# A two-stage kernel on one core: the filler products of TensorE at the start go from 26 to 44, with a new fixed order of the first half

## The chip, the cores and the metric

One Trainium2 chip, one of its cores. The metric is the device time of one launch in microseconds (us); lower is better. A core has five engines that each run their own instructions in the order of the program: PE (TensorE, matrix products, with its weight loads shown as PEld), DVE (VectorE), ACT (ScalarE), POOL (GpSimd) and SP (here it only issues transfers). Semaphores tie the engines together; an engine whose next instruction has to wait holds up everything behind it.

## What is computed

```python
# attention part: 4 batches x 8 heads, 768 steps, head size 48
k_n = k / (norm(k) + 1e-6)
for t in range(S):
    y[t]  = q[t] @ state
    v_old = state^T k_n[t]
    state = state + beta[t] * outer(k_n[t], v[t] - v_old)
# feed-forward part: x is y laid out as 3072 tokens x 384
h = x @ w_in          # 384 x 2048
g = h * cos(h)
out = g @ w_out       # 2048 x 384
```

All of it is float32. Nothing of it changes with the edit.

## The kernel before, in words

The sequence is cut into 24 units of 32 steps (`n` in the code); two units make a block of 256 tokens (`p`, 12 of them) for the feed-forward part. For each unit the recurrence is solved in closed form: `turn` (L556) transposes keys and queries on TensorE, `gram` (L588) makes their products, `gram_keys`, `fold` and `gram_queries` (L610, L631, L662) bring these out of the accumulators on VectorE, `inv` (L709) inverts a triangular matrix (on VectorE for the first pair of units, on GpSimd afterwards), `back` (L646) brings the inverse into place. Then comes the chain that runs from unit to unit: `state` (L752, keys and queries times the state), `old` (ACT), `right` (DVE), `solve_half` (L805), `half_out` (ACT), `between` (L813), `between_out` (DVE), `solve` (L825), `solve_out` (DVE, L843), `update` (L856), `update_out` (DVE, L868), which gives the state of the next unit, and beside it `within` (L874), `within_out` (ACT) and `within_rest` (DVE, both L888), which give the unit's output y. `features` (L899) transposes y, `features_out` (ACT, L909) lays it down as x. From there on the feed-forward part can use it: `hidden` (L956, x times w_in), `turns`, `rest`, `cos` and `gate` (g = h cos h on ACT and DVE), `out` (times w_out). From block 1 on the second product, and from block 2 on the first product as well, use sums of tiles to save multiplications (`layer`, `in_sums`, `right`, `left`, `collect`).

The weights come in as 64-bit words of which one float is wanted. Each of the 28 pieces takes a load on SP (`weights`, L450), two passes on ACT (`split`, L457), two on DVE (`shift`, L466) and one on POOL (`add`, L475). Four landing buffers hold the pieces, so a fifth load waits until an earlier `add` is done.

`busy` (L951) is a product of a constant tile that nobody reads. It writes to the accumulator of the output, which is not in use until the first `out`; the first `out` is ordered behind the last `busy` (L1604). One call is one product of 128x256, which the profile shows as two instructions. `BUSY` (L1303) is the number of calls.

The order of the work is not found by a scheduler at build time. All steps, with their dependencies, are registered by `order.add`, and `Order.run` (L175) issues them in the order that the list of numbers `LINE` (L54) gives; number i is the i-th step registered. The same list thus sets the order on each of the five engines, and which buffer a step gets: a tag of which all buffers are in use is passed on as soon as its last user in the list is done. Of the accumulators that matter here, `two` and `kq` exist once each, `h` three times (L1294 to L1297). Units 0, 2 and 4 are transposed and multiplied in `two`, units 1 and 3 in `kq`, so `turn` of unit 2 waits until the last reader of unit 0's products is done, and `solve_half` of unit 0 waits until the last reader of unit 2's products is done. The end of the function pins each engine's instructions to the order of issue.

The function that the list drives:

Of the kernel before, what the change touches and what calls it, by code (L numbers as in the profile page):

```python
# [54 lines left out]
0 1 2 3 4 5 6 7 2141 8 9 10 11 12 37 13 76 38 14 39 42 34 98 64 15 43 69 65 40 66 70 44 2145 45 99  # L55
67 71 2142 16 47 17 72 2143 2149 128 75 2144 2146 46 77 106 143 2153 201 129 18 101 74 19 2147 2150
20 78 2148 21 2157 165 22 102 23 79 103 2154 131 36 107 73 2155 136 2151 2156 24 137 2161 80 25 190
2158 26 132 104 27 133 28 81 2165 108 166 29 2152 109 2162 48 41 110 49 111 2169 2159 50 63 2163
2160 51 168 52 2166 169 30 2164 2173 53 191 134 54 170 31 2170 55 2167 56 2177 223 2171 58 68 2172
32 59 57 2174 60 172 2168 2181 100 138 2175 173 2176 33 139 61 142 2185 62 2189 743 171 130 144 2182  # L60
140 141 744 2178 248 82 2179 145 174 83 749 175 2183 2190 224 750 176 2191 2184 755 751 84 745 177
756 2186 2193 2192 226 2187 146 2197 85 281 746 86 87 752 747 88 748 89 2194 2188 90 753 757 227
2180 91 2198 2201 105 93 2205 2199 147 92 2195 194 94 2200 148 761 195 2209 2196 95 2202 196 758 228
2213 2206 762 197 199 198 759 2207 96 112 97 754 2210 2203 767 2208 2214 2211 200 2204 763 768 760
113 2215 2217 2212 230 2221 114 773 2225 231 2216 249 229 791 769 202 770 764 2229 135 765 167 115
2218 774 203 116 771 2222 772 117 775 779 2226 776 192 118 777 2227 204 119 766 780 120 306 121 781
2230 123 122 785 124 2219 205 782 786 125 783 339 784 126 778 149 787 127 788 252 150 2231 2220 789
819 2223 253 2228 151 820 2233 2237 2224 35 225 152 821 790 825 153 803 206 822 823 826 2241 2234
287 154 2235 827 283 831 155 824 288 156 804 2232 832 157 2242 2236 193 2238 2245 158 2243 207 833
837 364 159 828 232 834 829 160 284 792 161 233 811 835 208 162 2249 234 250 807 163 179 164 2239  # L70
2246 254 830 235 838 255 836 2250 257 843 839 2251 209 180 310 844 812 285 840 849 289 841 258 259
845 805 850 178 256 2244 2247 793 2252 846 181 847 346 2240 842 813 851 855 2248 848 898 309 182 260
852 856 183 853 854 184 210 857 251 186 286 261 794 187 185 397 899 341 900 211 795 188 868 797 212
808 262 858 859 213 901 282 214 861 215 860 216 189 902 263 218 422 904 862 219 217 905 798 909 317
863 220 903 906 221 290 815 264 345 799 311 399 342 291 292 800 222 864 912 865 809 265 866 796 312
400 801 307 237 313 907 867 314 920 923 315 921 810 870 347 266 932 293 908 934 933 911 873 924 910
938 935 914 940 874 922 939 915 238 913 941 267 916 367 936 871 876 942 937 343 925 943 872 947 926
869 236 949 878 948 944 957 239 945 950 879 816 951 316 946 880 818 802 344 368 955 806 817 240 956
881 952 882 268 241 318 953 954 242 308 244 404 960 245 243 319 884 958 917 961 455 269 959 246 962
992 270 886 927 963 971 883 320 928 887 964 271 965 403 369 272 966 888 967 273 968 247 321 930 274  # L80
931 889 969 276 480 875 970 885 277 977 972 275 890 978 278 973 979 877 814 322 891 974 279 980 975
426 348 929 375 976 295 349 981 986 892 982 919 894 280 987 323 983 988 895 918 984 350 296 893 985
989 425 998 990 896 991 370 324 993 1011 371 999 1045 373 1042 994 1006 1000 995 1007 1014 1043 996
351 1008 997 1009 1001 457 1054 1010 1002 1012 1056 1055 325 1003 401 374 297 1004 1044 1046 1058
1005 1057 1013 1062 1060 1047 1059 458 1069 1061 294 402 1071 1070 1017 1015 1063 433 1048 376 1072
340 1079 1064 1018 372 1065 405 1073 897 298 377 461 1020 299 1066 300 1074 1067 1022 302 326 1075
1016 1023 1068 303 378 1050 301 1077 365 304 327 1078 1076 1049 1080 1024 328 1053 513 1052 1019
1082 1025 379 1081 329 1026 1083 1084 330 1085 1028 331 1086 305 1087 332 1030 1088 380 366 334 538
1031 335 1089 333 1090 1029 1093 1091 336 1032 1092 1021 337 1094 1099 381 398 427 1095 406 1100 353
1096 1051 1097 407 423 1101 1033 354 1098 1034 1102 382 1027 338 1108 408 515 1103 1114 1109 1104  # L90
1035 1110 1105 462 355 1106 1111 1036 516 1038 1112 383 1107 1113 1039 459 1037 1115 409 1164 1116
1120 1167 1040 1117 428 1121 1165 1118 517 1128 1133 429 1129 1119 431 1122 1130 1131 1176 1123 352
1168 1136 1124 1132 1177 1125 1178 518 1126 432 1139 1166 1127 1180 483 1137 1179 430 1184 1182 1169
1181 1138 1191 1134 1183 1135 356 1192 434 491 1193 357 384 1185 1172 1194 1140 1170 1195 1186 484
1171 435 1187 1196 358 463 1197 360 1142 571 359 361 1198 1201 1188 436 460 1189 1199 385 1200 1190
1202 1204 1041 1144 1203 362 519 1145 1174 1205 1141 386 437 1206 1146 1175 1207 363 1208 1215 1147
520 1209 1148 1210 1211 1150 438 1149 387 1212 1152 456 1236 1213 1214 388 1216 1153 481 389 1217
1221 1218 439 485 1219 390 1222 392 596 1173 391 1223 393 1143 1154 1220 1224 440 1230 1155 1225
1156 394 1226 1231 395 1227 1157 1232 542 1151 1228 1233 573 1158 1229 1160 1234 1159 574 1235 396
1161 1237 575 464 441 465 1242 466 1238 1162 1239 486 1243 1286 467 1240 411 1250 1289 1251 1241  # L100
1244 1252 1255 487 1253 1245 489 1287 1246 1254 1258 1247 410 424 1298 1261 1248 1300 1299 1288 1249
412 490 521 1302 541 1301 1259 1304 488 1256 1262 1305 413 1303 1290 549 1291 1307 1260 1306 492 414
1308 1264 415 442 1309 1310 1313 1257 1311 493 1266 1315 1163 1314 1312 416 1316 1292 418 1317 629
1267 1318 417 1319 494 419 1323 1320 482 1321 1268 1322 1324 577 1326 1293 1325 420 1294 522 1269
1327 495 443 1328 421 523 578 1329 1270 543 1330 444 1272 524 1331 600 1337 1274 1332 496 445 1275
1333 1263 514 1334 1265 446 1335 1276 447 1336 599 1297 1338 1343 497 1277 1339 1271 448 1344 1295
525 1340 450 449 1341 1345 451 1342 539 1278 1346 1347 498 1352 1348 1279 1353 452 1354 1349 544 453
1280 1350 1355 1273 545 1282 547 546 1351 1356 1358 1296 1357 1378 454 1364 1359 1283 1365 1360 1372
548 1366 1361 1373 1284 1362 499 469 1374 1281 1367 1375 1377 1363 1408 1368 1409 1380 1376 550 1411
1369 1420 576 468 1422 1421 1370 1410 1412 1383 1371 470 551 1424 654 540 1384 1423 1413 471 1428  # L110
1386 579 1425 1426 1381 1379 472 1427 552 1435 500 473 1429 1382 1436 474 1430 635 1388 476 1431
1414 1389 1432 477 475 553 1285 1437 1385 687 1433 1387 1390 478 1438 501 1391 1439 1434 1415 1392
502 1416 1440 554 1443 1393 1441 1419 1445 1444 1442 1394 503 1446 572 1447 1448 1396 1418 1395 1397
1449 636 1450 555 504 1451 1398 505 1452 479 506 1399 1453 508 712 507 1454 556 1400 509 1455 601
1456 607 580 631 1457 1459 1458 581 510 1465 511 1460 583 632 1401 1466 1461 582 633 1467 1462 557
1417 1463 602 1468 512 527 1464 1402 603 1474 1469 1470 1404 605 1475 1471 1476 1405 1472 526 528
1473 1477 1406 1480 1478 606 1530 1486 1479 529 1481 1499 1403 1500 1487 657 1482 1531 1494 1488
1483 1495 1502 604 1484 1496 597 608 1485 1497 530 1533 1542 1498 1489 1544 1532 1407 1490 531 1543
609 1491 1505 532 637 1492 534 689 1493 693 1546 1545 1534 535 1506 1535 610 690 533 1548 1550 558
1547 1503 1508 1549 1501 665 1536 1551 1504 658 1510 1557 1552 536 559 611 1558 1509 1553 694 634  # L120
1559 560 1511 1560 1554 1561 1512 561 1555 1562 630 1556 1563 562 612 1565 1564 1513 1567 563 655
1566 1570 1538 1568 659 1514 1571 1569 537 1516 1572 613 715 1573 564 1574 1518 1575 566 1537 1576
1519 565 567 1577 614 1581 1578 568 569 1520 1579 1541 1580 1507 638 1582 1587 1517 1583 639 1584
585 1588 570 1515 1585 1589 1521 586 640 691 1539 1586 1602 1590 641 1596 1540 1591 1522 1597 615
# [76 lines left out]
def kernel(  # L201
# [1101 lines left out]
    BUSY = 26  # L1303
# [506 lines left out]
```

## Time and profile before

| what | us |
|---|---|
| three runs | 631.16, 634.62, 634.65 |
| their median | 634.62 |
| the profiled execution, whole | 634.23 |
| its span, from the first to the last instruction | 632.2 |
| TensorE products, busy in the span | 603.0 |
| VectorE, busy in the span | 545.6 |
| mean granted TensorE clock | 0.984 |

The page of the profile divides the span into 40 equal slices of 15.8 us; a digit is the busy share of an engine in tenths, and PEclk the granted clock of TensorE in tenths. The view by windows gives the same for stretches of one's own choice. The timeline lists an engine's instructions in order of time, merged when alike: start, length, engine, line, operation, tiles, number; in brackets the idle time of the engine before it and what ended it. A product in float32 counts as two instructions.

### The profile page before, as it was taken

To read this page: it belongs to the slowest core of one execution; us is meant where nothing else is said; L and a number is where in the kernel's file an instruction comes from. 1 tells how busy PE (TensorE), PEld (TensorE's weight loads), DVE (VectorE), ACT (ScalarE), POOL (GpSimd) and SP (SyncE) were. 2 spreads that over 40 slices of the span, in tenths; PEclk is the share of its full clock that TensorE was granted. 3 is DMA by queue.
4 is the path that set the end of the run, shared out by engine and by line. 5 is a ranking of instruction groups with operands and counts; after the bars stand their busy time and mean duration, and the time that the engine had idled before them with its cause. 6 is when DMAs were issued, how large, how long until landed. Compare 5 with 4: busy or idle time off the path is not lost.

```text
span 632.2 us, 24257 instructions
## 1 busy us (share of the span) xinstructions
PE 603.0 (95%) x10096; PEld 559.2 (88%) x10096; DVE 545.6 (86%) x1131; ACT 350.7 (55%) x643; POOL 345.8 (55%) x703
## 2 busy tenths in 40 slices
PE   7669799999999999999999999999999999999997
PEld 5458678877998989999999999999999999999996
DVE  6986978989999999988999998989988887878782
ACT  3644666554454756655655566755645655746340
POOL 4465787858948588387186683782680780000000
PEclk9877899999999999999999999999999999999999
DMA  9786574764454645555554445544334103110000
GB/s 180 189 215 155 140 182 107 130 101 78 85 102 82 127 77 102 99 85 104 89 87 92 92 75 112 104 72 74 70 77 82 48 17 66 34 42 22 1 26 25
DMA packets 223985, 57.60 MB, mean 91 GB/s; under 512 B 215684, under 2 KB 218900, under 8 KB 223876
## 3 DMA queue, kind: packets, MB, share of 16 engines
q1 hardware_dynamic: 221444, 55.22, 43.4%
q8 instruction: 79, 1.29, 0.9%
q10 hardware_dynamic: 2176, 0.39, 0.4%
q0 software_dynamic: 256, 0.45, 0.4%
q14 instruction: 30, 0.25, 0.1%
HBM read 42.13 MB, written 13.89 MB: 89 GB/s over the span
## 4 chain that ended last, share of the span: by engine, by line
PE 74%; DVE 10%; DMA 5%; ACT 3%; issue 2%; POOL 2%; SPq 2%; ACTq 0%; DVEq 0%
PE p_out L1226 28%; PE p_h L1149 27%; PE p_kq L764 3%; PE p_h L963 3%; PE p_s L862 3%; PE p_kq L879 2%; PE p_out L1169 2%; PE p_g L598 2%; PE p_u L841 2%; DMA pairs<-in_moe_w_in_dram 2%; DMA qp<-in_q_dram 2%; PE p_o L1226 2%; DVE p_h L1047 1%; SPq L339 1%; DVE pairs L468 1%
## 5 line engine op out<-in xcount | busy, mean ns | idle before, releaser
L734 POOL TENSOR_TENSOR part<-z,gb 128x56 f32<-128x56 f32 (+25 forms) x325 | 134.3, 413 | 113.5 <-DMA gb<-g_dr 58.1
L735 POOL TENSOR_TENSOR z<-z,part 128x56 f32<-128x56 f32 (+25 forms) x325 | 138.2, 425 | 25.5
L1165 ACT COPY g_ffn<-p_h 128x512 f32<-128x512 f32 x140 | 79.7, 586 | 90.3 <-DVE p_h L1047 49.5
L1226 PE MATMUL p_out<-w_out,g_ffn 128*128 128x192 f32 x672 | 120.9, 329 | 0.0
L1047 DVE TENSOR_TENSOR p_h<-p_h,g_ffn 128x512 f32<-128x512 f32 x140 | 97.0, 695 | 18.9 <-ACT g_ffn L1165 10.9
L1226 PEld LDWEIGHTS p_out<-w_out,g_ffn 128*128 128x128 f32 x672 | 107.9, 191 | 0.7
L1001 ACT ACTIVATE turns<-p_h,quarter_turn 128x512 int32<-128x512 f32 x96 | 65.8, 687 | 64.2 <-DVE p_h L1047 52.8
L1017 ACT ACTIVATE turns<-turns,halfpi 128x512 f32<-128x512 f32 x96 | 69.2, 722 | 46.9 <-DVE turns L1008 45.7
L1226 PE MATMUL p_out<-w_sum,g_ffn 128*128 128x192 f32 x496 | 91.2, 331 | 0.5 <-DVE p_h L1047 0.5
L1149 PE MATMUL p_h<-x_sum,w_in 128*128 128x128 f32 x640 | 83.9, 278 | 0.4 <-ACT g_ffn L1165 0.3
L1226 PEld LDWEIGHTS p_out<-w_sum,g_ffn 128*128 128x128 f32 x496 | 79.4, 190 | 2.2 <-DVE p_h L1047 0.6
L1149 PEld LDWEIGHTS p_h<-x_sum,w_in 128*128 128x128 f32 x640 | 78.1, 192 | 1.9 <-ACT g_ffn L1165 1.0
L1008 DVE SCALAR_TENSOR_TENSOR turns<-p_h,turns 128x512 f32<-128x512 f32 x96 | 65.3, 684 | 8.1 <-ACT turns L1001 7.7
L1242 DVE TENSOR_TENSOR g_ffn<-g_ffn 128x512 f32<-128x512 f32 x88 | 62.7, 722 | 4.1 <-PE p_out L1226 3.9
L1026 DVE TENSOR_TENSOR g_ffn<-turns,p_h 128x512 f32<-128x512 f32 x86 | 58.4, 680 | 6.8 <-ACT turns L1017 6.7
L1149 PE MATMUL p_h<-x_sum,in_sum 128*128 128x128 f32 x400 | 53.8, 278 | 0.7 <-DVE g_ffn L1026 0.6
L897 ACT COPY y<-p_kq 32x384 f32<-32x384 f32 x88 | 41.3, 469 | 19.0 <-PE p_kq L879 13.6
L963 PE MATMUL p_h<-x_ffn,w_in 128*128 128x128 f32 x384 | 50.3, 289 | 1.1 <-ACT x_ffn L912 0.7
L1149 PEld LDWEIGHTS p_h<-x_sum,in_sum 128*128 128x128 f32 x400 | 49.5, 192 | 2.0 <-DVE g_ffn L1026 0.6
L963 PEld LDWEIGHTS p_h<-x_ffn,w_in 128*128 128x128 f32 x384 | 46.9, 201 | 2.7 <-issue 1.1
L776 ACT COPY rhs<-p_kq 32x384 f32<-32x384 f32 x86 | 40.2, 467 | 7.8 <-issue 4.9
L1149 PE MATMUL p_h<-x_ffn,w_in 128*128 128x128 f32 x320 | 42.9, 278 | 0.1
(133 smaller groups left out, 891.4 us busy)
## 6 DMA issues: line engine op xcount, KB each, us to landing
pairs<-in_moe_w_in_dram SPq DMA_DIRECT2D x12, 512.0 KB, 3.9
pairs<-in_moe_w_out_dram SPq DMA_DIRECT2D x16, 384.0 KB, 4.2
gb<-g_dr SPq DMA_DIRECT2D x20, 256.0 KB, 3.6
vp<-in_v_dram SPq DMA_DIRECT2D x96, 48.0 KB, 2.4
out_dram<-o SPq DMA_DIRECT2D x23, 192.0 KB
y_dr<-y_t SPq DMA_DIRECT2D x20, 192.0 KB, 3.4
x_ffn<-y_dr SPq DMA_DIRECT2D x40, 96.0 KB, 2.5
kp<-in_k_dram SPq DMA_DIRECT2D x128, 24.0 KB, 2.2
```

What stands on the lines that cost most here:

```text
L734: eng.tensor_tensor(out=part, in0=row, in1=times, op=ALU.mult)
L735: eng.tensor_tensor(out=behind, in0=behind, in1=part, op=ALU.subtract)
L963: nc.tensor.matmul(p_h[:, i], w_in[:, t, (4 * k + i) * 128 : (4 * k + i + 1) * 128], moved(p, t, unit), start=(t == 0), stop=(t == KT - 1),)
L1001: nc.scalar.activation(turns[p, f], hidden_of(p, f), AF.Identity, bias=quarter_turn, scale=TURN)
L1008: nc.vector.scalar_tensor_tensor(out=r, in0=hidden_of(p, f), scalar=TURN, in1=t, op0=ALU.mult, op1=ALU.subtract,)
L1017: nc.scalar.activation(r, r, AF.Sin, bias=halfpi, scale=2.0 * math.pi)
L1026: nc.vector.tensor_tensor(out=place(p, f), in0=step_of(rests.pop((p, f)), f), in1=step_of(hidden_of(p, f), f), op=ALU.mult,)
L1047: nc.vector.tensor_tensor(out=out, in0=one, in1=two, op=ALU.add if op == "add" else ALU.subtract)
L1149: nc.tensor.matmul(p_h[:, e], in_block(w)[:, e], form(p, x), start=first and e == 0, stop=True, skip_group_check=True,)
L1165: nc.scalar.copy(block(p, *CHAIN[i][3]), p_hs[p, BANK[i]])
L1226: nc.tensor.matmul(p_o, left(p, part, a)[:, e % 4], right(e, b), start=(e == 0), stop=(e == FT // 2 - 1), skip_group_check=True,)
L1242: nc.vector.tensor_tensor(out=left(p, s, to), in0=left(p, s, one), in1=left(p, s, two), op=op)
```

## The change

`BUSY` becomes 44, which registers 18 more steps, so that every number in `LINE` from 34 on means another step. The list is written anew. Put back into names, its last 1191 entries (from about block 4 on) are the same steps in the same order as before; of the 1036 steps ahead of these that are not `busy`, 959 stand in another place, 745 of the 1036 within 10 places of the old one and 985 within 40. No step's own code is touched, and the dependencies are the same.

```
     VECTOR = {0: "h"}
-    BUSY = 26
+    BUSY = 44
...
-0 1 2 3 4 5 6 7 2141 8 9 10 11 12 37 13 76 38 14 39 42 34 98 64 15 43 69 65 40 66 70 44 2145 45 99
+0 1 2 3 4 5 6 7 2159 8 9 10 11 12 55 13 56 60 57 52 116 82 87 61 83 58 84 88 62 2163 63 117 94 85 89
...
```

In names, TensorE's order up to the features of unit 1 (BUSYxN are N products that nobody reads, `hidden.p,f,part`):

```
before: BUSYx7 turn.0 BUSYx1 turn.1 gram.0 gram.1 BUSYx2 turn.2 BUSYx6 turn.3 BUSYx5 gram.2 BUSYx1 state.0
  solve_half.0 between.0 BUSYx1 solve.0 BUSYx1 update.0 within.0 BUSYx1 turn.4 gram.3 BUSYx1 features.0
  hidden.0,0,0 hidden.0,0,1 state.1 gram.4 hidden.0,2,0 hidden.0,2,1 hidden.0,4,0 hidden.0,4,1 solve_half.1
  between.1 solve.1 update.1 within.1 turn.5 hidden.0,6,0 gram.5 hidden.0,6,1 features.1
after:  BUSYx6 turn.0 turn.1 gram.0 gram.1 BUSYx21 turn.2 BUSYx3 turn.3 BUSYx2 gram.2 BUSYx6 state.0 BUSYx2
  solve_half.0 between.0 solve.0 BUSYx2 update.0 within.0 turn.4 gram.3 features.0 BUSYx1
  hidden.0,0,0 hidden.0,0,1 hidden.0,2,0 gram.4 state.1 hidden.0,2,1 hidden.0,4,0 solve_half.1
  between.1 solve.1 hidden.0,4,1 update.1 within.1 turn.5 hidden.0,6,0 BUSYx1 gram.5 state.2 hidden.0,6,1 features.1
```

(`state.0` issues nothing: the state is zero.) VectorE's order over the same stretch, up to the end of unit 0's output:

```
before: sum.0,0 beta sum.0,1 scale.0,0 gram_keys.0 scale.0,1 gram_queries.0 gram_keys.1 shift.0 cross.0 fold.0
  inv.0,0 gram_queries.1 shift.1 inv.0,1 sum.1,0 inv.0,2 fold.1 shift.3 shift.2 inv.0,3 sum.1,1 scale.1,0 back.0
  gram_keys.2 weigh.0,0 fold.2 right.0 gram_queries.2 shift.4 shift.5 sum.2,0 between_out.0 scale.1,1 solve_out.0
  shift.6 shift.7 weigh.0,1 update_out.0 within_rest.0
after:  sum.0,0 beta sum.0,1 scale.0,0 gram_keys.0 scale.0,1 fold.0 gram_keys.1 gram_queries.0 cross.0 sum.1,0
  inv.0,0 shift.0 inv.0,1 shift.1 shift.2 scale.1,0 gram_queries.1 fold.1 shift.3 inv.0,2 sum.1,1 gram_keys.2
  inv.0,3 weigh.0,0 back.0 fold.2 gram_queries.2 right.0 shift.4 shift.5 between_out.0 shift.6 sum.2,0 scale.1,1
  solve_out.0 shift.7 update_out.0 beta_home within_rest.0
```

ACT, after `within_out.0`: before `split.8 turn_out.4 features_out.0 split.10 split.9 old.1`, after `turn_out.4 split.9 features_out.0 split.10 split.11 turns.0,0 split.12 old.1`; `split.8` now stands ahead of `within_out.0`. POOL: `norms.1,0` now stands ahead of `add.0`, `add.9` and `add.10` ahead of most of `inv.1`. SP: `q.3` now goes ahead of `k.3`, `v.0` ahead of `weights.4`, `q.5` and `q.6` ahead of `weights.8` and `weights.9`; `v.1`, `k.6` and `v.3` go later.

## The prediction

> **What bounds the kernel now.** First the page: busy times, the slices, the clock. Then windows, to see which stretch loses what; then the timelines of TensorE and VectorE over the begin.
>
> ```profile
> span 632.2 us, 24257 instructions
> PE 603.0 (95%) x10096; PEld 559.2 (88%) x10096; DVE 545.6 (86%) x1131; ACT 350.7 (55%) x643; POOL 345.8 (55%) x703
> ...
> PE   7669799999999999999999999999999999999997
> ...
> DVE  6986978989999999988999998989988887878782
> ...
> PEclk9877899999999999999999999999999999999999
> ```
>
> TensorE is the bound from the fifth slice on; only the begin has pauses and a clock below full. A gain must come from the first 100 us, and it lasts to the end, since what TensorE does earlier is not waited for again.
>
> ```profile
> 30.00:40.00 10.00, 5.38 (x195) 4.32 (x196) 9.11 (x25) 4.79 (x8) 7.52 (x5) 0.74 0.86 218
> 40.00:50.00 10.00, 7.55 (x181) 5.51 (x181) 8.44 (x20) 4.76 (x12) 5.51 (x6) 0.84 0.81 188
> 50.00:60.00 10.00, 10.00 (x179) 9.63 (x179) 5.21 (x12) 3.51 (x8) 5.74 (x16) 0.74 0.60 144
> 60.00:70.00 10.00, 6.82 (x284) 5.96 (x283) 8.39 (x16) 6.95 (x13) 8.15 (x17) 0.94 0.61 165
> ```
>
> Columns: length, busy us and instructions of PE, PEld, DVE, ACT, POOL, then granted clock, DMA share, GB/s. From 30 to 40 us VectorE is full and TensorE is not; from 50 to 60 us TensorE is full at three quarters of the clock and VectorE idles half the time. Read in half-microsecond windows, the clock is 0.5 from 17.7 to 21.1, 34.8 to 41.6, 48.4 to 55.25 and 68.9 to 72.3, and 1.0 afterwards: 20.5 us at half clock, so 10.2 us of TensorE's work lost. All edges lie multiples of 3.41 us apart.
>
> ```profile
> 13.42 1.13 PE L954 MATMUL p_out<-eye 128*128 128x256 f32 x4
> 17.71 1.08 PE L561 MATMUL p_t<-consts,kp 128*128 128x128 f32 x4 [3.16 <-DVE part_v L734]
> 25.19 0.63 PE L561 MATMUL p_t<-consts,kp 128*128 128x128 f32 x4 [1.95 <-issue]
> 26.10 2.32 PE L954 MATMUL p_out<-eye 128*128 128x256 f32 x10
> 33.91 0.88 PE L801 MATMUL p_w<-vp,halves_z 32*32 32x48 f32 x64 [4.08 <-issue]
> 46.84 0.66 PE L598 MATMUL p_g<-kq_t 48*32 48x64 f32 x41 [1.09 <-issue]
> 49.12 5.46 PE L963 MATMUL p_h<-x_ffn,w_in 128*128 128x128 f32 x24 [0.66 <-ACT x_ffn L912]
> 54.51 1.46 PE L764 MATMUL p_kq<-st,kq_t 48*64 48x48 f32 x64
> ```
>
> ```profile
> 26.54 1.52 DVE L473 TENSOR_SCALAR w_in<-w_in 128x512 uint32<-128x512 uint32 x1
> 33.41 0.40 DVE L664 TENSOR_TENSOR tt<-p_g,consts 128x256 f32<-128x256 f32 x1
> 39.73 1.02 DVE L849 TENSOR_TENSOR u<-p_u,bz 128x384 f32<-128x384 f32 x2 [0.61 <-PE p_u L835]
> 44.04 1.13 DVE L895 COPY y<-p_kq 32x384 f32<-32x384 f32 x2
> 56.79 0.42 DVE L624 TENSOR_TENSOR g<-p_g,bs 128x256 f32<-128x256 f32 x1 [4.45 <-PE p_g L598]
> ```
>
> Each of TensorE's pauses up to 44 us ends with a VectorE step: turn.2 at 17.71 follows fold.0, turn.3 at 25.19 follows fold.1 (24.81 to 25.09), solve_half.0 at 33.91 follows gram_queries.2 (33.41 to 33.81). VectorE itself waits 0.61 us for TensorE before solve_out.0 (39.73), and 4.45 us before 56.79: that is where the half clock hurts, because 24 product instructions (5.46 us; later rows of 24 at full clock take 2.9) stand ahead of state.1 and gram.4.
>
> **The change, part by part.** *The 18 added products.* Ten instructions at full clock take 2.32 us, the last one 0.38: (2.32 - 0.38)/9 = 0.216 each, 0.43 per product. At the start 14 took 6.29, so 0.85 per product at half clock. The block of 21 begins at about 13.4 and lasts 42 x 0.216 = 9.1 us, to 22.5: turn.2 comes at 22.5 instead of 17.71. Behind it on TensorE: turn.2 (0.9), 3 products (1.3), turn.3, which needs fold.1 at about 25.2 as now, so that the queue is idle again: 25.2 to 26.1; 2 products to 27.0; gram.2 to 27.8. Its reader gram_keys.2 on VectorE has inv.0,2 and sum.1,1 ahead of it and is reached at about 28.5. Slack 0.7 us: cost nothing, as long as the block runs at full clock. At half clock until the gate opens it is 1.7 to 3.4 us longer, and 1.0 to 2.7 of it would reach VectorE. The 6 + 2 products after gram.2 end at 27.8 + 8 x 0.43 = 31.2, ahead of solve_half.0. The 6 instead of 7 at the start only wait for loads less long. Of the 18, then, nothing lies on the path, and what they hold up, the clock between 17.7 and 41.6 us, is worth little: VectorE waited 0.61 us for it in all (39.73). Gain 0 to 0.6.
>
> *VectorE up to the first output.* Summing durations in both orders, the work up to gram_queries.2 is the same. But two of its rows were stretched beside a POOL add: L473 at 26.54 took 1.52 where others take 0.42, and the sum of cross.0 0.99 where cross.1's took 0.43. In the new order POOL's adds fall elsewhere (add.0 behind norms.1,0, shift.2 next to no add). Gain 0 to 1.66; I take 1.1, so solve_half.0 at 32.8. From there to the end of within_rest.0 now 11.36 us; weigh.0,1 leaves (0.47), beta_home comes (0.78), the wait of 0.61 goes, and of the second stretched L473 (35.26, 1.52) about half: 10.5 to 11.7, I take 11.2. So within_rest.0 ends at 44.0 instead of 45.17.
>
> *To the first hidden product.* Now 45.17 to 49.12 = 3.95: gram.3 with a pause of 1.09 inside it (46.84), one product, p_z, x on ACT. The product goes behind features.0 (-0.4), but split.9 (1.25) stands ahead of features_out.0 on ACT, and split.8 ahead of within_out.0. Their loads wait for landing buffers: weights.9 for the sixth add at about 37.3, and behind q.6 on SP (1.88), so 39.5; early loads took up to 7.3 us from issue to their split (13.24 to 20.53): 46.8 at worst, 44.2 by the issue at 21.45 and the next piece of the chain ending at 26.16. Taken: hidden.0 at 47.0; ends 46.0 and 49.2.
>
> *The clock under these products.* Between 37.7 and 46 us the new order leaves TensorE update, within, turn.4, gram.3, features.0 and one product: about 4.5 us of 9, longest pause about 2.2. Windows of 3.41 us ahead of the four drops held 0.3, 0.8, 2.1 and 1.5 us of busy TensorE; ones with 1.9 and more were also kept. So I expect a drop here as now, and the gate to open after a whole busy window: at about 52, half clock for some 5 us of products instead of 6.1. Gain 0.5 in TensorE's work.
>
> *Unit 1.* state.1 now comes after 12 more product instructions and gram.4: from 47.0, 22 instructions at 0.228 to 52, 14 at 0.118 to 53.7, gram.4 0.8, state.1 from 54.5 to 55.7 (now 55.97). old.1 to 56.7. right.1 was reached at 60.24 because shift.10, gram_queries.4 and shift.12 (1.02 + 0.42 + 1.81) stood between it and 56.79; now only gram_keys.4 does. right.1 at 56.8, 1.73 long, then gram_queries.4: solve_half.1 at 59.0 instead of 62.23. From there to features.1 now 14.15 us; hidden.0,4,1 put ahead of update.1 (1.4) lies beside solve_out.1 (1.1), back.1 moves behind within_rest.1 (1.8 earlier), shift.15 and sum.3,0 come ahead of it (about 1.8): nil.
>
> *Sum.* Start of hidden.0 -2.1, clock -0.5, the order after it -0.6: unit 1 stands 3.2 us earlier at features.1, and TensorE, 9 tenths or more busy from there to the end, keeps it. Later moves (in_sums, right, left, stores, loads by up to 50 places; q.3, v.0, q.5 ahead on SP and v.1, k.6, v.3 behind) I cost at nothing: by sums of durations VectorE's work ahead of features.2, update_out.5 and the products of block 2 differs by less than 3.1 us either way while TensorE's own queue is 95% full; if that cover is gone, the difference is the price. 634.23 - 3.2 = 631.0; the profiled execution is 0.39 below the median of 634.62.
>
> **A rule against it.** The row first: the drop at 48.4 came after a window (45.0 to 48.4) with 2.1 us of busy TensorE. The Trainium skill (TensorE: Matmul & The Clock Gate, What's actually happening) says that the clock goes to half after at least one idle window of about 3.4 us. By that rule this drop would not have come, so the trace disagrees here. By it the new begin, whose longest pause I put at 2.2 us, would stay at full clock: that is the first rival.
>
> **Rivals.** (1) The clock holds through the first features. For it: 1.9 us of busy TensorE in a window were sometimes enough. Against: 2.1 were not. The 24 + 12 instructions then take 4.2 instead of 6.7, and the rest of the 10.2 us lost now stays away: 631.0 - 2.5 - 1.7 (68.9 to 72.3) = 626.8. (2) Slower: state.1 behind 12 more instructions at half clock. It decides if hidden.0 does not start earlier than 49.1, through the pause of 1.09 or a late weights.9. Then 36 instructions at 0.228 end at 57.3, gram.4 0.8, state.1 at 58.1 against 54.51; VectorE's next steps wait and unit 1 is 3.6 late: 637.8, or 636 if right.1's shorter queue gives half back. (3) It does nothing: the pauses end with VectorE, which is full, and the later order gives the rest back: 634.2.
>
> **How the numbers follow.** Forecast 0.42 (its own range 629 to 633), rival 1 0.2, rival 2 0.2, rival 3 0.18. Leaving out a tenth on each side: 626.0 to 638.0. One per cent, about what a measurement of this kernel can tell from no change, is 6.3 us: faster means below 628.3, slower above 641.0. Rival 1 and the low tail of the forecast give 0.22; slower by more needs rival 2 and another unit lost the same way, 0.08; within 0.70.
>
> **What would show it.** In the new profile: turn.2 near 22.5 and gram_keys.2 without an idle bracket (the block is covered); solve_half.0 near 32.8; within_rest.0 ending near 44.0; the first hidden product near 47.0; a half clock over it but not from 17.7 to 41.6; solve_half.1 near 59; features.1 near 73. I am wrong if gram_keys.2 waits for TensorE, if hidden.0 starts at 49 or later, or if pauses on TensorE appear after 100 us that were not there.

## The result: 1.4% slower

| | us | runs |
|---|---|---|
| before | 634.37 (630.92 to 634.81) | 6 |
| after | 641.22 (637.58 to 643.87) | 6 |
| after by before | 1.0142, 95% interval 1.0111 to 1.0173 | |

The profiled execution of the changed kernel took 641.66, its span 639.9. The forecast was 631.0, its upper end 638.0. The page of the changed kernel:

```profile
span 639.9 us, 24344 instructions
PE 613.7 (96%) x10132; PEld 570.4 (89%) x10132; DVE 547.7 (86%) x1131; ACT 351.2 (55%) x643; POOL 347.9 (54%) x703
...
PE   7959889999989999999999999999999999999997
...
DVE  6986779899979999998999998989988977878782
...
PEclk7977799999989999999999999999999999999999
...
q8 instruction: 80, 1.31, 0.9%
```

TensorE has 36 more product instructions, and the clock is lower in the first and fifth slices and in the twelfth. By windows of half a microsecond it is at half from about 9.4 to 16.2, 36.7 to 43.5, 46.9 to 57.1, 67.4 to 74.2 and 183.4 to 186.9, some 34 us against 20.5. The last line becomes important below: a queue that carries instructions moved 80 packets, 1.31 MB, 16 KB each. The four stretches shown of the kernel before, now of the changed one (same columns):

```profile
30.00:40.00 10.00, 5.65 (x185) 4.51 (x187) 9.07 (x17) 4.83 (x8) 4.98 (x4) 0.83 0.83 172
40.00:50.00 10.00, 6.30 (x136) 5.10 (x135) 7.90 (x19) 2.19 (x4) 6.55 (x4) 0.67 0.79 197
50.00:60.00 10.00, 9.82 (x171) 8.62 (x170) 6.34 (x18) 6.56 (x14) 6.04 (x12) 0.64 0.44 126
60.00:70.00 10.00, 7.39 (x293) 6.76 (x281) 7.84 (x15) 5.35 (x10) 6.20 (x14) 0.87 0.57 123
```

From 40 to 50 us TensorE does 136 products where it did 181. The timeline of TensorE says why:

```profile
13.75 10.52 PE L955 MATMUL p_out<-eye 128*128 128x256 f32 x42
24.10 0.60 PE L562 MATMUL p_t<-consts,kp 128*128 128x128 f32 x4
...
28.10 0.86 PE L599 MATMUL p_g<-kq_t 48*32 48x64 f32 x64
...
34.60 0.88 PE L802 MATMUL p_w<-vp,halves_z 32*32 32x48 f32 x64 [1.99 <-issue]
...
39.89 0.85 PE L836 MATMUL p_u<-u_half,halves_z 32*32 32x48 f32 x28 [1.12 <-issue]
40.67 2.08 PE L955 MATMUL p_out<-eye 128*128 128x256 f32 x4
42.73 1.23 PE L863 MATMUL p_s<-u,kp 64*64 64x96 f32 x32
43.89 0.88 PE L880 MATMUL p_kq<-u,tt 32*32 32x48 f32 x64
48.47 1.09 PE L562 MATMUL p_t<-consts,kp 128*128 128x128 f32 x4 [3.69 <-DMA vp<-in_v_dram]
...
53.29 6.09 PE L964 MATMUL p_h<-x_ffn,w_in 128*128 128x128 f32 x36
...
65.49 0.88 PE L802 MATMUL p_w<-rhs,halves_z 32*32 32x48 f32 x64 [1.37 <-DVE tt L665]
```

solve.0 breaks off in the middle for 1.12 us, and turn.4 (48.47) starts 3.69 us after within.0 has ended. The label of the second pause names a load that turn.4 doesn't use; its keys, its queries and its buffer were there by 45.06, when update_out.0 ended. Count what lies between the two pauses: 28 + 4 + 32 + 64 = 128 products, and each is two instructions, a weight load and a product (the page has x10132 of both). 256 instructions lie from one pause to the next. Before the change the pause of 1.09 in gram.3 and the next one without a wait, in solve.1, lie three times 256 apart, when the waits that stand as instructions of their own in TensorE's queue are counted too:

```profile
66.23 0.80 PE L835 MATMUL p_u<-u_half,halves_z 32*32 32x48 f32 x56 [0.67 <-issue]
```

VectorE beside it:

```profile
23.14 1.29 DVE L520 TENSOR_TENSOR krec<-knrm 128x8 f32<-128x8 f32 x1
...
29.00 0.63 DVE L618 TENSOR_TENSOR w_sum<-p_g,bh 128x128 f32<-128x128 f32 x2
...
30.77 1.61 DVE L550 TENSOR_TENSOR vp<-vp,knrm 128x384 f32<-128x384 f32 x1
...
38.22 1.52 DVE L474 TENSOR_SCALAR w_in<-w_in 128x512 uint32<-128x512 uint32 x1
...
46.56 1.13 DVE L896 COPY y<-p_kq 32x384 f32<-32x384 f32 x2
...
51.56 0.63 DVE L618 TENSOR_TENSOR w_sum<-p_g,bh 128x128 f32<-128x128 f32 x2 [2.81 <-PE p_g L599]
```

gram_keys.2 (29.00) has no bracket: the block of 21 is covered, as forecast, though VectorE came to it 0.5 us later than forecast. The rows stretched beside a POOL add are others now (L520, L550, again one L474), and are as long. within_rest.0 starts at 46.56, and VectorE waits 2.81 us for gram.3 behind turn.4.

Comparing the time at which TensorE has done the same number of useful products (those that nobody reads left out), the profiled execution is 4.2 us late at 50 us, 4.2 at 120, 2.9 at 178, 6.3 at 185, 7.8 at 280, 7.7 at the end: the begin, a step at 180, a small one near 264. Since the orders differ in between, these are good to about 1 us.

### The profile page after: what moved, and what is told of

Its sections match the earlier page's. It is cut to its first block, busy times and chain, and to the rows that moved or that the text cites. A ratio compares the mean times of both kernels' runs of the same rounds, so it can differ in the third digit from the quotient of the medians.

```text
span 639.9 us, 24344 instructions
## 1 busy us (share of the span) xinstructions
PE 613.7 (96%) x10132; PEld 570.4 (89%) x10132; DVE 547.7 (86%) x1131; ACT 351.2 (55%) x643; POOL 347.9 (54%) x703
## 3 DMA queue, kind: packets, MB, share of 16 engines
q8 instruction: 80, 1.31, 0.9%
## 4 chain that ended last, share of the span: by engine, by line
PE 72%; DVE 9%; POOL 7%; DMA 4%; issue 3%; SPq 2%; ACT 1%; DVEq 0%; POOLq 0%; ACTq 0%
PE p_out L1227 26%; PE p_h L1150 26%; PE p_h L964 3%; PE p_kq L765 3%; POOL part L735 3%; POOL z L736 3%; PE p_out L955 3%; PE p_s L863 2%; PE p_kq L880 2%; PE p_g L599 2%; PE p_u L842 2%; DMA kp<-in_k_dram 2%; PE p_o L1227 2%; PE p_t L562 1%; DVE p_h L1048 1%
## 5 line engine op out<-in xcount | busy, mean ns | idle before, releaser
L1009 DVE SCALAR_TENSOR_TENSOR turns<-p_h,turns 128x512 f32<-128x512 f32 x96 | 65.1, 683 | 11.9 <-ACT turns L1002 11.5
L964 PE MATMUL p_h<-x_ffn,w_in 128*128 128x128 f32 x384 | 51.2, 291 | 0.0
L507 POOL TENSOR_TENSOR knrm<-ksum,halves 128x16 f32<-128x16 f32 (+1 forms) x14 | 36.0, 2575 | 14.6 <-DVE ksum L495 9.2
```

The costliest lines, as they stand in the source:

```text
L964: nc.tensor.matmul(p_h[:, i], w_in[:, t, (4 * k + i) * 128 : (4 * k + i + 1) * 128], moved(p, t, unit), start=(t == 0), stop=(t == KT - 1),)
L1009: nc.vector.scalar_tensor_tensor(out=r, in0=hidden_of(p, f), scalar=TURN, in1=t, op0=ALU.mult, op1=ALU.subtract,)
```

## The experiments

**Theory F.** TensorE's instructions come as packets of 256. In the trace's records of the instruction queue, with the end of the pause behind each:

```
before  packet 44.11 to 45.40   gram.3 goes on at 46.84   (1.44 later)
after   packet 36.65 to 38.44   solve.0 goes on at 39.89  (1.45)
after   packet 45.70 to 46.72   turn.4 starts at 48.47    (1.75)
after   packet 89.94 to 91.09   between.2 goes on 92.33   (1.24)
```

18 products are 72 instructions. They move the end of every later packet; one that lay in gram.3 (pause 1.09) comes to lie in front of turn.4 (3.69). **Theory S** stands for the step at 180: SP issues get.6 late. (`put` and `gram_put` store a pair's inverse and a unit's products in DRAM, `get` loads a unit's part of the inverse back; `solve` of that unit needs it.) The rivals are named with each run. In all that follows "over before" is the ratio to the kernel before, measured beside it, less one. The profiled runs of one kernel differ among themselves, so the ratios decide and profiles show places.

**Experiments 1 to 4.** First, before's order with 18 products in its pauses:

```diff
+BUSYx7 ahead of turn.2, BUSYx4 ahead of turn.3, BUSYx7 ahead of state.0   # before's LINE otherwise
```

> The kernel before, in its own order, with 18 more products put where its TensorE waits: 7 ahead of turn.2, 4 ahead of turn.3, 7 ahead of state.0. In its trace these pauses are 3.16, 1.95 and 4.08 us, the products 0.43 each. Theory F (TensorE's instructions come in packets of 16 KB, 256 instructions, and TensorE stops at the end of a packet when the next one is late): the 72 added instructions put the end of a packet, which lay inside gram.3 (pause 1.09), at turn.4, as in the changed kernel, where the pause was 3.70; expected 635.5 to 638. Theory N (products are free, the new order alone costs): 634.4 within 1, no pause over 1.2 us at turn.4.

Measured: 638.44, 0.92% over before (0.66 to 1.19). N falls: the products alone cost most of it. within.0 now breaks off one product ahead of its end for 2.33 us, and gram breaks off at 124.72 for 2.17. The next two leave the new order as it is and replace products by small ones:

```diff
-for _ in range(parts): nc.tensor.matmul(flat_out[:, 0 : HC * HC], eye16[:, 0:128], eye16)
+size, times = (32, TINY[parts]) if parts in TINY else (128, 1)     # parts: number of the product
+for z in (slice(size * (s % 4), size * (s % 4) + size) for s in range(times)):
+    nc.tensor.matmul(flat_out[z, 0 : 2 * size], eye16[z, 0:size], eye16[z, 0 : 2 * size])
+TINY = {6: 17}                       # second run; {6: 17, 7: 17, 8: 17} in the third
```

> The changed kernel, with one of the 21 products ahead of turn.2 replaced by 17 small ones (32x32 weights, 64 columns, nobody reads them): 64 more TensorE instructions, some 0.2 us more time in a pause. Theory F: ends of packets move 64 instructions forward, from the middle of solve.0 and turn.4 to the start of solve.0 and the middle of within.0; turn.4 follows within.0 within 1 us and the pause of 3.70 at turn.4 is gone, one of 0.5 to 3 appears inside within.0; first hidden product 0 to 3 us earlier, 638 to 641. Theory W (turn.4 waits for an operand, a buffer or a load): turn.4 starts at 48.5 as before, 641.

Measured: 636.46, 0.71% over before (0.40 to 1.02), half of the change's cost gone by 64 instructions that do nothing; 638 to 641 was expected. turn.4 starts at 44.01 with 0.32 idle ahead of it. W falls by the time, not by this one profile: the fourth run, with no shift, has no pause at turn.4 either. The pauses are elsewhere, and not quite where expected: 0.94 in solve.0 and 1.82 ahead of gram.3.

> As the shift by 64, but three products replaced by 51 small ones: 192 more TensorE instructions. Theory F: ends of packets at row 372 (between.0), 500 (the two products ahead of update.0) and 628 (middle of gram.3) instead of solve.0 and turn.4: turn.4 without a pause over 1 us, a pause of 1 to 3 us inside gram.3 or at the two products; 637 to 641. Theory W: turn.4 at 48.5 with its 3.7 us, 641.

Measured: 640.53, 1.19% (0.68 to 1.70). turn.4 has no pause, but the small products ran out of instructions themselves (2.30 us at 16.57) and held solve_half.0 up to 37.70. It decides nothing about the place in the chain.

```diff
-put.3 gram_put.8 store.0,1 get.6        # SP's order
+put.3 get.6 gram_put.8 store.0,1
```

> The changed kernel with one load moved in SP's queue: get.6 right behind put.3, ahead of gram_put.8 and store.0,1, as the order before had it. Theory S: solve.6 waits at 182.72 for that load, issued at 178.06 behind gram_put.8 (3.62 us of issue) and the store; it then starts at 179 to 180, the half clock from 181.4 to 184.85 goes, and the time falls by 2.5 to 4 us, to 637 to 638.5. Rival: what comes next (inv.3, 2.6 us later on GpSimd than before, or VectorE) holds solve.6 as long; 640.5 to 641.5.

Measured: 640.56, 1.17% (0.81 to 1.54), against 1.42 (1.11 to 1.73): too close to tell. In the profile the place is mended. SP's and TensorE's timelines, the changed kernel first:

```profile
173.23 0.38 SPq L740 DMA_DIRECT2D z_dr<-z  x1
173.65 3.62 SPq L683 DMA_DIRECT2D g_dr<-g  x3
177.37 0.58 SPq L1288 DMA_DIRECT2D out_dram<-o  x1
178.06 1.89 SPq L748 DMA_DIRECT2D zt<-z_dr  x4
```

```profile
182.72 0.28 PE L842 MATMUL p_u<-rhs,zt 64*64 64x48 f32 x2 [1.47 <-DMA zt<-z_dr]
183.33 1.82 PE L842 MATMUL p_u<-rhs,zt 64*64 64x48 f32 x30 [0.33 <-DMA zt<-z_dr]
185.08 1.99 PE L1150 MATMUL p_h<-x_sum,in_sum 128*128 128x128 f32 x8
```

And with get.6 put forward:

```profile
176.23 1.79 SPq L748 DMA_DIRECT2D zt<-z_dr  x4
178.07 1.74 SPq L683 DMA_DIRECT2D g_dr<-g  x3
```

```profile
179.06 0.31 PE L842 MATMUL p_u<-rhs,zt 64*64 64x48 f32 x2
179.65 1.10 PE L842 MATMUL p_u<-rhs,zt 64*64 64x48 f32 x30 [0.27 <-DMA zt<-z_dr]
```

get.6 (L748) stood behind a gram_put that took 3.62 us to issue and a store. With it forward, solve.6 does not wait at its start, and the products behind it run at full clock. The same run lost 3.80 us at 88.67, in front of the same product of between.2 at which the changed kernel paused for 1.98. Theory S is shown for the place; its worth in the whole time is taken up below.

**Experiments 5 to 8.** They separate products, begin and middle, and measure the supply of instructions by itself.

```diff
-BUSYx21 turn.2        # after's LINE otherwise
+BUSYx3 turn.2
```

> The changed kernel, its new order kept, with 18 of the 21 products ahead of turn.2 taken out: 26 products as before. Theory F: the ends of packets lie 72 instructions further on, no longer at turn.4 but some 36 rows behind it, in gram.3; a pause of 1 to 2 us there; begin 0 to 4 us earlier than in the changed kernel, but the waits from 170 us on stay: 636 to 640. If the new order alone costs all of it: 641. If the products alone do: 632 to 634.

Measured: 636.06, 0.59% over before (0.23 to 0.95). So the 18 products cost 0.92 in the old order and 1.42 - 0.59 = 0.83 in the new one. The packet's end expected inside gram.3 makes no stop there in this profile.

```diff
+steps of after's LINE up to update_out.5, then the steps left in before's order     # 6
+steps of before's LINE up to update_out.5, then the steps left in after's order     # 7
```

> The changed kernel's order up to update_out.5 (some 156 us, with its 44 products), and from there on the order before for the steps that are left. Theory M (of the 7.7 us, 3.5 come at 170 to 185 us and 1.5 at 262 to 280, from the new order of the middle): these go, 635 to 637, no wait of solve.6 for its load. Rival (all of it is the begin, the middle only shows it): 640 to 641.

> The order before up to update_out.5 with its 26 products, then the changed order for the steps that are left. Theory M: solve.6 waits for get.6 behind gram_put.8 and the stores, and 262 to 280 loses 1.5: 636 to 639. Rival (all is the begin): 633 to 635.

Measured: 636.57, 0.66% (0.35 to 0.97), and 634.65, 0.41% (0.12 to 0.69). By the ratios both give a part. The second time, 634.65, lies in the rival's range of 633 to 635; but the kernel before, measured beside it, took 632.03, and the ratio's interval leaves out zero. In the first the pause at turn.4 is back (3.49 at 46.78). In the second the profiled run loses about 1 us from 160 to 165 and about 1.7 from 258 to 280; the waits of TensorE there are 0.79 for VectorE (159.77) and 0.34 for the load of solve.10 (259.74). solve.6 did not wait for its load in that run, which theory M had named.

```diff
+TINY = {0: 769}       # before's LINE
```

> The kernel before, with its first product replaced by 769 small ones (32x32 weights, 64 columns; 1538 rows of TensorE, 3076 instructions, 12 packets of 16 KB and the 4 of the product), to measure the supply of instructions by itself: rows of this kind took 0.0172 us in groups of 64. Theory F: bursts of 128 rows (2.2 us at full clock) with a pause of 1 to 3 us at the end of each packet, each ending 1.2 to 1.75 us after a transfer of 16 KB on the instruction queue: 40 to 60 us for all. Rival (transfers of instructions are ahead of TensorE anyway): 26 to 30 us without pauses.

Measured: from 1.35 to 49.65 us for the small products, 671.46 in all. TensorE's timeline:

```profile
20.45 1.99 PE L954 MATMUL p_out<-eye 32*32 32x64 f32 x128 [1.19 <-issue]
24.46 1.99 PE L954 MATMUL p_out<-eye 32*32 32x64 f32 x128 [2.02 <-issue]
27.91 1.99 PE L954 MATMUL p_out<-eye 32*32 32x64 f32 x128 [1.47 <-issue]
31.37 1.99 PE L954 MATMUL p_out<-eye 32*32 32x64 f32 x128 [1.47 <-issue]
35.37 2.70 PE L954 MATMUL p_out<-eye 32*32 32x64 f32 x128 [2.02 <-issue]
39.10 5.90 PE L954 MATMUL p_out<-eye 32*32 32x64 f32 x256 [1.02 <-issue]
```

This is the mechanism bare: 128 products, a pause, 128 products, a pause, with no other engine in play; "issue" means that no wait is on record. From 26 us on the DMA share is 0.04 and less, so these pauses need no other transfer. Where the work takes 1.99, it is 3.45 to 4.01 us from one start to the next. The pauses end 1.3 to 1.7 us after a packet's end (one 0.84). The next packet starts 1.0 to 2.4 us after TensorE went on, which fits a packet that is asked for only when the one before it is begun. In the last line two packets pass without a pause, since at half clock, up to 43.3, the work takes longer (5.90 for both). F stands: 256 instructions that TensorE could run in less than the 3.45 to 4.01 us of this run make it wait. Numbered with the waits in TensorE's queue, the stops of this run stand at instructions 448, 704, 960 and so on, those of the changed kernel at 960, 1219 (behind turn.4's own waits) and 3009: each within three of 192 more than a multiple of 256. The chain of a unit is full of such runs (64 products in 0.8 to 0.9 us), the feed-forward products are not (128 of them take 15 us).

The Trainium skill (Perfetto Trace Analysis, The 4-stage abstract model) says that an instruction has 64 bytes; the trace agrees, 16,384 bytes by 256. The Trainium skill (Trainium Architecture — The Big Picture, The software stack) has the instruction streams brought into each engine's memory when the program is loaded. If that sentence means the whole stream, the trace disagrees: 80 packets of 16 KB came during the execution, about as many as the 20,264 weight loads and products of TensorE need (79.2), and TensorE waited for some.

**Experiments 9 to 12.** Is it the place of the packets, or the products?

```diff
+TINY = {1: 19}                       # 9: before's LINE
+TINY = {1: 17, 2: 16, 3: 16}         # 10: the LINE of the first experiment
```

> The kernel before with the shift of the 18 products but without their time: one of the seven products at the start is replaced by 19 small ones, 72 more TensorE instructions, no step moved. Theory F (what the 18 products cost is where they put the ends of TensorE's packets of 256 instructions): as the kernel before with 18 products, 636 to 639. Theory P (the products' own time, or the clock under them): 632 to 633, as before.

> The kernel before with the 18 products of the first experiment and, in place of three products at the start, 49 small ones: 256 more TensorE instructions behind these, one whole packet, so that all later ends of packets lie where they lay before. Theory F: 632 to 634. Theory P: 637 to 639, as with 18 products alone.

Measured: 637.13, 0.83% over before (0.54 to 1.11), with no product more, no step moved; and 634.41, 0.31% (0.05 to 0.57), with all 18 products and a whole packet added. TensorE in the ninth run breaks off at the same product as in the first:

```profile
43.87 1.50 PE L879 MATMUL p_kq<-u,tt 32*32 32x48 f32 x63
48.16 0.23 PE L879 MATMUL p_kq<-u,tt 32*32 32x48 f32 x1 [2.80 <-issue]
```

P falls but for 0.3%: the 18 products cost most of what they cost by the 72 instructions that they put into the stream. The small products are not a cost by themselves, as the thirteenth run shows below. The next two ask why the packet at turn.4 came so late.

```diff
-weights.8 q.6 weights.9 v.1 weights.10 v.2 weights.11 weights.12 k.6      # 11: after, SP
+weights.8 weights.9 weights.10 v.1 v.2 weights.11 weights.12 q.6 k.6
-weights.8 q.5 weights.9 k.6 weights.10 v.2 weights.11 weights.12 v.3      # 12: before, SP
+weights.8 weights.9 weights.10 q.5 v.2 weights.11 weights.12 v.3 k.6
```

> The changed kernel with two loads moved back in SP's queue: q.6 from ahead of weights.9 to behind weights.12, v.1 from behind weights.9 to behind weights.10. Nothing waits for them before 56 us. Theory F with its cause (the packet of instructions queues behind loads: the DMA share was 0.8 to 1.2 from 39 to 44 us and the packet came at 45.7, when it fell to 0.4): the packet for turn.4 comes at 40 to 42, turn.4 has no pause over 1 us, weights.9 lands sooner; 636 to 639. Rival (the lateness of a packet is no matter of loads): turn.4 pauses by 3 us, 641.

> The kernel before with the same kind of edit: q.5 from behind weights.8 to behind weights.10, k.6 from behind weights.9 to behind v.3. The packet at 44.11 had a DMA share of 0.8 to 1.0 ahead of it and gram.3 a pause of 1.09 behind it. Theory F with its cause: the packet comes at 42, the pause goes, hidden.0 starts at 47 to 48; 629 to 632, a little faster than before. Rival: 632 to 633, as before, or later if the moved loads are then late for turn.5.

Measured: 637.19, 1.09% (0.79 to 1.40), and 632.29, 0.06% (-0.10 to 0.22). In the eleventh run the packet comes at 42.33 instead of 45.70 and the pause at turn.4 is 1.30 instead of 3.69; the whole time moves the same way, within the intervals. In the twelfth the packet comes at 42.75 instead of 44.11 and gram.3 runs through. That begin is 3.8 us ahead at 55 and loses 2.6 by 65: VectorE waits 2.54 us for a split at 57.32, and TensorE 1.67 for VectorE at 60.06. Both packets came earlier, as expected, but that it was the loads is not shown. In the fourth run, with no load of the begin moved, the packet of turn.4 came at 38.63, at a DMA share of 0.98; in the seventh, with the begin of before unchanged, that of gram.3 came at 43.32. And neither move changed the whole time by more than its uncertainty.

**Experiments 13 to 15.** Can the place be reckoned ahead?

```diff
+TINY = {1: 13}                       # 13: before's LINE
+TINY = {1: 33}                       # 14: before's LINE
+TINY = {6: 21}; get.6 behind put.3, get.10 behind put.5      # 15: after's LINE
```

> The kernel before with 13 small products in place of one at the start: 48 more TensorE instructions, no step moved. Reckoned from the rows of the run that has the order before up to 156 us: a packet of 128 rows that TensorE runs through in less than 4.1 us (6 while the loads of the begin fill the queues) makes up the difference as a pause. By that sum the pauses are 3.9 us as it stands, 1.9 for a shift of 48 (the least of 16 shifts tried on paper) and 7.5 for 128 (the most). Theory F: 629 to 632, the same as before or up to 2 us faster. Rival (any shift is worse than the one that the order was made with): 635 to 638, as the shift by 72.

> The kernel before with 33 small products in place of one at the start: 128 more TensorE instructions, the worst of the shifts by the same sum (pauses of 1.4 at 39, 2.1 at 42, 2.0 at 52, 1.8 at 113 us, 7.5 in all against 3.9). Theory F: 636 to 641, pauses at these places. Rival (the shift by 72 was bad for another reason): 631 to 634.

> The changed kernel with get.6 behind put.3 and get.10 behind put.5 in SP's queue, and 80 more TensorE instructions (one of the 21 products replaced by 21 small ones), the place with the least pauses by the same sum. Theory F with theory S: the packets give back 0.5 to 0.7 per cent as the shift by 64 did, the two loads 2 to 3.5 us: 631 to 634, as the kernel before. If the new begin is worth the 5.8 us that the profiled run of the shift by 64 had in hand at 140 us: 627 to 630, faster than both. If the loads are not it: 636, as the shift by 64.

Measured: 633.51, 0.07% (-0.18 to 0.33); 641.50, 1.23% (0.74 to 1.72); 642.52, 1.60% (1.10 to 2.09). The bad place came out bad, by 7.8 us where the sum gave 3.6; the good one is as before, where the sum gave a gain of 2. So the sum tells a bad place from a harmless one here, and no more. The stops at a packet's end, added up over the whole profiled execution, do not rank the runs either: 2.2 us before and 6.8 in the changed kernel, 5.4 in the ninth run and 11.5 in the fourteenth, but also 4.6 in the tenth and 4.2 in the thirteenth, which cost 0.31 and 0.07%. Where TensorE would have waited anyway, a stop can cost nothing; which of these did was not worked out. Of the four pauses named for the fourteenth run two came, somewhat later (2.49 at 56.96, where gram of another unit breaks off, and 1.15 at 119.61); those at 39 and 42 did not, and others did (1.89 at 126.68, 2.24 at 309.23).

```profile
53.68 0.79 PE L598 MATMUL p_g<-kq_t 48*32 48x64 f32 x56
56.96 0.32 PE L598 MATMUL p_g<-kq_t 48*32 48x64 f32 x8 [2.49 <-issue]
```

The fifteenth is a miss, and of my making. SP and TensorE of it:

```profile
250.40 0.52 SPq L740 DMA_DIRECT2D z_dr<-z  x1
253.60 3.27 SPq L748 DMA_DIRECT2D zt<-z_dr  x4
```

```profile
266.46 2.04 PE L1150 MATMUL p_h<-x_ffn,in_sum 128*128 128x128 f32 x8 [5.63 <-DVE g_ffn L1027]
```

get.10 (L748) waits until put.5 has landed, from 250.92 to 253.60, and SP with it. store.2,0 and what is behind it come later, ACT waits 6.99 us for the store's buffer, VectorE for ACT, TensorE 5.63 for VectorE. It was 2.5 us ahead of the kernel before at 260 and 4.8 behind at 280. A packet still stopped between.0 for 2.96 us.

**Experiments 16 to 18.** Do the costs add?

```diff
+TINY = {6: 17}; after's LINE to update_out.5, then before's order      # 16
+BUSYx3 turn.2;  after's LINE to update_out.5, then before's order      # 17
+TINY = {6: 17}; get.6 behind put.3                                     # 18: after's LINE
```

> The changed order with its 44 products up to update_out.5, the order before behind it, and the packets shifted by 64 instructions as in the second experiment. If the costs add (packets 0.7 per cent of the change's 1.4, the middle 0.4 to 0.7): 0 to 0.3 per cent over the kernel before, 631 to 635. If the new begin with well placed packets is worth what the profiled run of the shift by 64 had in hand at 140 us: 627 to 630, faster than both kernels. If the packets' place in the begin is no separate cost: 636 to 637, as without the shift.

> The changed order without the 18 products up to update_out.5, the order before behind it. The changed order without the 18 products whole was 0.6 per cent over the kernel before. If that is the middle: 631 to 634. If it is the new begin: 635 to 637.

> The changed kernel with the packets shifted by 64 instructions and get.6 behind put.3, get.10 left where it is. If the costs add: 0.71 per cent less 0.1 to 0.4 over the kernel before, 634 to 637, with no wait of solve.6 for its load. If get.6 is worth nothing in the whole time: 637.

Measured: 635.40, 0.49% (0.27 to 0.70); 633.42, 0.17% (-0.03 to 0.37); 636.31, 0.63% (0.38 to 0.87). Per cent over before, all together:

| order | 26 products | 44 | 44, shift 64 |
|---|---|---|---|
| before | 0 | 0.92 | |
| new begin, middle of before | 0.17 | 0.66 | 0.49 |
| begin of before, new middle | 0.41 | | |
| new | 0.59 | 1.42 | 0.71 |

The columns give the 18 products 0.92, 0.49 and 0.83; the rows give the new middle 0.41, 0.42, 0.76 and 0.22, and the new begin 0.17 and 0.18 where the products are left out. From the kernel before by way of its new middle and the new order with 26 products they add to 1.4: 0.4 middle, 0.2 begin, 0.8 products. They depend on each other: with 44 products the new begin is 0.26 below the old one, whose products stand elsewhere, and the shift by 64 gave 0.71 back in the new order but 0.17 with the middle of before. get.6 alone is 1.42 to 1.17 and 0.71 to 0.63, within the uncertainty both times. None of the 18 beats the kernel before.

## Why the prediction was wrong

- **The added products, costed at nothing.** The local part held: the block ended at 24.27 instead of 22.5, and gram_keys.2 did not wait. The step that failed is "of the 18, then, nothing lies on the path". It priced their time and not their instructions. 72 instructions move every later end of a packet, and in the order before that alone costs 0.83% (experiment 9), 5.3 us, where the 18 products with a whole packet's worth of instructions cost 0.31% (experiment 10).
- **The pause of 1.09 in gram.3, taken as given.** It stood in the fence with the label "issue" and went into the sum as a fixed part of 3.95 us. It was the end of a packet. The second rival named it as a possible cause of lateness, and the condition of that rival was met: the first hidden product started at 53.29, not at 47.0. Its 3.6 us are near the 4.2 that the profiled execution is late at 120; the rest came behind 178, which it costed at nothing.
- **VectorE up to the first output: gain of 1.1.** Failed: other rows stretch, solve_half.0 came at 34.60 and not 32.8 (before 33.91). That beta_home would cost 0.78 was low as well: L416 and L417 took 1.43. within_rest.0 ended at 47.70, with the pause of 1.12 in solve.0 and one more L474 of 1.52 ahead of it, instead of 44.0.
- **The clock.** A drop was expected over the first features, 5 us of it; it lasted from about 46.9 to 57.1 and began in the pause ahead of turn.4. So the first rival, a clock that holds, failed. The clock was also at half from 183.4 to 186.9, behind the wait for get.6.
- **Unit 1.** With the first hidden product 6.3 us late all follows: solve_half.1 at 65.49 instead of 59.0, features.1 at 81.76 instead of 73. Up to solve_half.1 the stretch took 12.2 us, as forecast (12.0). From there to features.1 it took 16.27 instead of 14.15; that term, put at nil, was 2.1 short. The clock was at half there from 67.4 to 74.2, before from 68.9 to 72.3; what the new order has to do with it was not separated.
- **"Later moves … I cost at nothing."** Wrong by 0.4%, 2.6 us (experiment 7). Sums of VectorE's work and TensorE's fullness were no cover for a load that SP issues in order: get.6 was behind 3.62 us of issue. The sign that I had named, pauses on TensorE after 100 us that were not there, is what the trace shows at 182.72. That one load explains the step of some 3.4 us at 180 in the profiled execution (0.4 with it put forward), not the 0.4%: moving it gave 0.25 and 0.08, both within the uncertainty, and the run that priced the middle lost its time at other waits.

What stays open: how late a packet comes in one execution (turn.4 paused 3.69, 3.49, 1.30 and not at all in runs with the same TensorE order), which makes a single profile a poor judge here; whether loads decide it; which waits of the middle make its 0.4%; and whether the 0.2% of the begin is there at all, as its interval takes in zero.

## What to carry to other kernels

Where TensorE stops without a semaphore behind it, count the instructions from one stop to the next: if it is a fixed number or a multiple of it, as the 256 here, suspect the supply of instructions, and test it by adding instructions earlier: the stops must move. Filler that is free in time need not be free in instructions; the price of a filler is told only by a run with the same number of instructions and next to no time, and one with a whole packet more. In a queue that issues in order, cost a moved transfer by the issue time and the waits of what is now ahead of it, and before moving it forward ask what it waits for itself.

## What the runs showed of the hardware

TensorE's instructions came in packets of 16 KB, 256 instructions, during the execution. Small products were supplied at 256 instructions per 3.45 to 4.01 us, though TensorE could run them in 1.99, and with the DMA queues all but empty too. A stop ended mostly 1.2 to 1.75 us after the packet had landed. The packet for turn.4 started at 45.70, when the DMA share had fallen from 0.8 and more to 0.4; 3.4 us earlier with two loads moved, at a share of 0.13; and 7.1 us earlier in a run with none moved, at 0.98. Moving the stream by 72 or 128 instructions, with no step moved, changed the whole time by 0.83 and 1.23%; by 48, not measurably.
